# Converting float64 weights to float32: a scaled Abs and a maximum ahead of the shift in place of a guard behind the addition

## The chip, the cores and the metric

The kernel runs on one core of a Trainium2 chip. The metric is the time of the whole program on the device, in microseconds (us), as the median of several runs. The core's engines are TensorE (PE in the profile; PEld is its loading of weights), VectorE (DVE), ScalarE (ACT), GpSimd (POOL) and SyncE (SP), which here issues all transfers. Each works through its own queue in order.

## What is computed

```python
q_pool = q.reshape(B, H, S // 2, 2, D).mean(axis=3)        # B 4, H 8, S 1152, D 64
scores = np.matmul(q_pool, k.transpose(0, 1, 3, 2)) / np.sqrt(D)
attn = np.exp(scores - scores.max(-1, keepdims=True))
attn = attn / (attn.sum(-1, keepdims=True) + 1e-09)
x = np.matmul(attn, v)              # then as 2304 tokens of 512
h = x @ moe_w_in;  x = np.maximum(0.01 * h, h) @ moe_w_out          # 512 -> 2048 -> 512
h = x @ moe2_w_in; out = np.where(h > 0, h, np.exp(np.minimum(h, 0)) - 1) @ moe2_w_out
```

The attention inputs are float32. The four weight matrices arrive as float64, and the kernel computes in float32, so it converts them from their bits: each number is two 32-bit words, the low and the high one.

## The kernel before

The attention runs over 16 pairs (batch b of 4, head pair hp of 4). For each pair, `scores` (L452 to L463) multiplies queries by keys, takes the row maximum (DVE, L457 and L459) and the exponentials (ACT, L463); `transpose_p` (L475) turns the exponentials around and splits them into a rounded part and a rest (`psplit`, L261 to L267); `pv` (L496 to L509) multiplies by the values; `normalise` (L520 to L546) divides by the sums. L520 comes once for each pair, so its 16 instances mark how far the attention is.

The two layers of the MLP (`mlp`) run for each batch of 576 tokens over 16 blocks f of 128 hidden units: `up` (PE at L629, then the activation at L640 to L651), and after every four blocks `down` (PE at L667, sums on DVE at L680). Layer 0 and layer 1 of a batch are scheduled along with the attention of later batches. Each block needs 128 columns of w_in and 128 rows of w_out, tiles `wr` of 128 x 512, which `load_w` makes. When a layer's block is used for the first time (batch 0), `convert` makes it from the float64 words, and the result is also stored to memory (L328); later batches load that (`wr<-w`). ACT and POOL then split `wr` into `wi` or `wo` (L261, L267).

`convert` takes half a block (128 x 256) at a time, so there are 2 layers x 16 blocks x 2 matrices x 2 halves = 128 passes. Tiles `cr` (the raw words), `ct` and `cm` exist twice each (`CB = 2`). Per half the kernel before has six steps: on DVE the high word is shifted left by three and masked (L293), then its sign and top exponent bit are put in (L296); on ACT the low word is scaled by 2^-29 and so rounded (L299), and the magnitude of the high word, read as a float32, is taken into `cm` (L301); POOL adds the two words as integers (L303); on DVE the sum is multiplied by 1 or 0, as `cm` is at least `MIN_HI` or not, and written to `wr` (L305). That last step is the guard: numbers too small for the float32 exponent become zero.

The order on the engines is set by a planner inside the kernel (`Program`): every operation is entered with an engine, a cost in ns, a rank and the tiles that it reads and writes, and a list schedule decides the order in which they are emitted. A change of a step's engine, cost or inputs thus moves other instructions too. The costs of the steps concerned are

```python
def act(n, accum=False, sbuf=False):
    return 50 + 0.833 * n + (190 if accum else 0) + (43 if sbuf else 0)
def dve(n, fast=False):
    return 66 + (0.52 if fast else 1.05) * n
```

## Time and profile before

| | |
|---|---|
| three runs, median (lowest to highest) | 1552.36 us (1551.68 to 1554.34) |
| the profiled execution, first to last instruction (span) | 1550.8 us, 1.56 us under the median of the runs |
| PE busy | 1421.8 us, 92% |
| PEld busy | 1368.2 us, 88% |
| DVE busy | 1093.0 us, 70% |
| ACT busy | 1027.4 us, 66% |
| POOL busy | 844.7 us, 54% |
| granted TensorE clock, mean | 0.987 of full speed |

Busy shares are averages over a program whose first 590 us convert weights and whose rest does not; the shares of single stretches say more. Durations of an instruction include time in which it was begun and held up.

### The profile page before, as it was taken

What the parts mean: (1) busy time and instruction counts of PE and PEld (TensorE: products, weight loads), DVE (VectorE), ACT (ScalarE), POOL (GpSimd) and SP (SyncE); (2) the same over time, 40 slices, a digit from 0 to 9 for tenths busy, and PEclk for the clock granted to TensorE, in tenths of its full rate; (3) what the DMA queues carried; (4) which work ended last, traced back from release to release, by engine and by line L of the source; (5) the groups of instructions that cost most, each with busy time, mean ns of one, the idle gap of its engine ahead of it and who ended that gap; (6) DMA issues with size and microseconds to landing.
All of it is one profiled execution on the core that took longest, in us unless ns stands there. A gap on an engine that the chain in (4) does not pass through costs nothing.

```text
span 1550.8 us, 28885 instructions
## 1 busy us (share of the span) xinstructions
PE 1421.8 (92%) x10288; PEld 1368.2 (88%) x10288; DVE 1093.0 (70%) x2401; ACT 1027.4 (66%) x2773; POOL 844.7 (54%) x840
## 2 busy tenths in 40 slices
PE   5878899889888888999999999999999998899998
PEld 5777788878777788999999998999999998899897
DVE  6998898989999999656676767556676664224333
ACT  6998888777677777676667766776667652442442
POOL 5444256666666667444455556454554445566572
PEclk9999999999999999999999999999999999999999
DMA  4232124433334443222222222222221111322230
GB/s 145 90 114 86 40 79 139 128 114 124 125 119 136 142 133 115 83 77 60 69 74 70 79 77 63 93 73 61 70 71 42 55 55 56 92 76 82 69 89 31
DMA packets 82641, 135.58 MB, mean 87 GB/s; under 512 B 8512, under 2 KB 26944, under 8 KB 82496
## 3 DMA queue, kind: packets, MB, share of 16 engines
q1 hardware_dynamic: 82496, 133.73, 28.4%
q8 instruction: 81, 1.33, 0.4%
q14 instruction: 64, 0.52, 0.1%
HBM read 112.20 MB, written 21.50 MB: 86 GB/s over the span
## 4 chain that ended last, share of the span: by engine, by line
PE 50%; DVE 13%; ACT 3%; issue 2%; DMA 2%; POOL 2%; SPq 0%; ACTq 0%; POOLq 0%; DVEq 0%
PE h L667 15%; PE h L629 12%; PE s L452 5%; PE o L496 5%; PE t L475 4%; PE s L629 2%; DVE t L648 2%; PE s L667 2%; PE t L629 2%; DVE wr L305 2%; PE t L667 2%; DVE t L651 1%; PE t L373 1%; DVE pt L267 1%; DVE m L457 1%
## 5 line engine op out<-in xcount | busy, mean ns | idle before, releaser
L667 PE MATMUL h<-g,wo 128*128 128x288 f32 x2544 | 442.1, 305 | 18.5 <-DVE t L651 10.8
L629 PE MATMUL h<-xs,wi 128*128 128x288 f32 x2520 | 428.2, 305 | 22.9 <-DVE t L651 9.7
L629 PEld LDWEIGHTS h<-xs,wi 128*128 128x128 f32 x2520 | 362.8, 191 | 35.7 <-DVE t L651 15.4
L667 PEld LDWEIGHTS h<-g,wo 128*128 128x128 f32 x2544 | 368.6, 190 | 23.9 <-DVE t L651 13.0
L457 DVE TENSOR_REDUCE m<-s 128x1 f32<-128x384 f32 x432 | 231.3, 550 | 53.0 <-PE s L452 50.0
L267 POOL TENSOR_TENSOR g<-t,g 128x288 fp32r<-128x288 f32 x256 | 218.9, 863 | 89.3 <-ACT g L261 85.6
L261 ACT ACTIVATE pt<-t 128x384 fp32r<-128x384 f32 (+1 forms) x416 | 183.0, 455 | 126.1 <-PE t L475 116.4
L463 ACT ACTIVATE p<-s,m 128x384 f32<-128x384 f32 x432 | 248.4, 585 | 23.1 <-DVE m L459 22.7
L267 DVE TENSOR_TENSOR pt<-t,pt 128x384 fp32r<-128x384 f32 (+1 forms) x416 | 206.1, 508 | 56.6 <-ACT pt L261 55.0
L267 POOL TENSOR_TENSOR wo<-wr,wo 128x512 fp32r<-128x512 f32 x128 | 168.3, 1321 | 136.0 <-ACT wo L261 126.9
L452 PE MATMUL s<-kT,qT 128*128 128x384 f32 x768 | 195.2, 353 | 27.9 <-ACT p L463 27.6
L267 POOL TENSOR_TENSOR wi<-wr,wi 128x512 fp32r<-128x512 f32 x128 | 171.4, 1339 | 62.4 <-ACT wi L261 50.6
L475 PE MATMUL t<-ident,p 128*128 128x128 f32 x1116 | 181.1, 276 | 19.4 <-DVE pt L267 13.2
L496 PE MATMUL o<-pt,vn 128*128 128x256 f32 (+1 forms) x1152 | 190.7, 301 | 4.4 <-DVE pt L267 2.5
L496 PEld LDWEIGHTS o<-pt,vn 128*128 128x128 f32 x1152 | 164.4, 189 | 8.4 <-DVE pt L267 5.6
L261 ACT ACTIVATE g<-t 128x288 fp32r<-128x288 f32 x256 | 112.7, 446 | 88.1 <-DVE t L651 50.0
L475 PEld LDWEIGHTS t<-ident,p 128*128 128x128 f32 x1116 | 137.9, 142 | 31.5 <-DVE pt L267 14.1
L642 DVE SCALAR_TENSOR_TENSOR t<-t 128x288 f32<-128x288 f32 x128 | 90.6, 714 | 97.1 <-ACT t L640 96.6
L303 POOL TENSOR_TENSOR ct<-ct,cr 128x256 uint32<-128x256 uint32 x128 | 98.8, 773 | 109.5 <-DVE ct L296 41.0
L452 PEld LDWEIGHTS s<-kT,qT 128*128 128x128 f32 x768 | 126.1, 192 | 35.9 <-ACT p L463 34.5
L267 POOL TENSOR_TENSOR vn<-raw,vn 128x576 fp32r<-128x576 f32 x32 | 45.9, 1436 | 166.2 <-ACT vn L261 166.2
L261 ACT ACTIVATE wo<-wr 128x512 fp32r<-128x512 f32 x128 | 80.3, 630 | 83.0 <-PE h L667 51.8
(104 smaller groups left out, 2091.6 us busy)
## 6 DMA issues: line engine op xcount, KB each, us to landing
wr<-w SPq DMA_DIRECT2D x192, 256.0 KB, 2.7
cr<-in_moe_w_in_dram SPq DMA_DIRECT2D x64, 256.0 KB, 2.7
cr<-in_moe_w_out_dram SPq DMA_DIRECT2D x64, 256.0 KB, 2.7
w<-wr SPq DMA_DIRECT2D x64, 256.0 KB, 2.1
raw<-in_k_dram SPq DMA_DIRECT2D x32, 288.0 KB, 3.1
raw<-in_v_dram SPq DMA_DIRECT2D x32, 288.0 KB, 3.0
raw<-in_q_dram SPq DMA_DIRECT2D x32, 256.0 KB, 3.0
out_dram<-cr SPq DMA_DIRECT2D x16, 256.0 KB, 2.2
```

Source lines behind the costliest of these rows:

```text
L261: prog.add("ACT", act(n, sbuf=not psum), rank, lambda: A.activation(out=hi(), in_=src(), func=ACTF.Copy), w=[w], r=r)
L267: lambda: eng.tensor_tensor(out=lo(), in0=src(), in1=f32(hi()), op=ALU.subtract),
L303: prog.add("POOL", pool(CW), rank, lambda t=t, r=r: G.tensor_tensor(out=t.ap, in0=t.ap, in1=r[:, :, 0], op=ALU.add), w=[t], r=[t, (r, 0)])
L305: prog.add("DVE", dve(CW), rank, lambda n=n, t=t, mag=mag: V.scalar_tensor_tensor(out=dst[:, n:n + CW], in0=mag.ap, scalar=MIN_HI, in1=t.a ...
L452: PE.matmul(out=st[:, 0:384], lhsT=qa(a), rhs=kT[:, 384 * c:384 * c + 384], start=(i == 0), stop=(i == len(seq) - 1))
L457: prog.add("DVE", dve(384), rank - LR, lambda st=st, c=c: V.tensor_reduce(out=m[:, c:c + 1], in_=st[:, 0:384], axis=AX.X, op=ALU.max), w=[ ...
L463: prog.add("ACT", act(384, True), rank - LE, lambda c=c: A.activation(out=p[:, 384 * c:384 * c + 384], in_=banks[c][:, 0:384], func=ACTF.E ...
L475: PE.transpose(out=t[:, i, :], in_=p[:, (3 * c + i) * 128:(3 * c + i + 1) * 128], identity=ident)
L496: PE.matmul(out=o[:, 0:n], lhsT=vn[:, c, :], rhs=pt[th][:, a, c % 3, :], start=(c == 3 * ORDER[0] and a == 0), stop=(c == 3 * ORDER[2] + 2 ...
L629: PE.matmul(out=h[:, 0:HB], lhsT=wi[:, a, c, :], rhs=xs[c][:, e, cols], start=(c == 0 and a == 0 and e == 0), stop=(c == DC - 1 and a == 1))
L642: prog.add("DVE", dve(HB), rk, lambda t=t, g32=g32: V.scalar_tensor_tensor(out=g32.ap, in0=t.ap, scalar=0.01, in1=t.ap, op0=ALU.mult, op1= ...
L667: PE.matmul(out=y[:, 0:HB], lhsT=w[f][1][:, a, d * 128:(d + 1) * 128], rhs=g[f][:, e, cols], start=(f % FC == 0 and a == 0 and e == 0), st ...
```

## The change

The Abs pass on ACT now comes first. It multiplies by 2^16 and writes to `ct` in place of `cm`. A new DVE step takes the maximum of that and 2.0, in place. The shift by three works on the result in place, with a mask that keeps the top exponent bit; the next step adds the sign alone. The rounding of the low word is as before. POOL's addition now writes `wr` itself; the guard on DVE behind it and the tile `cm` are gone. Docstrings and comments, which the diff also removes, are left out here.

```diff
-    MIN_HI = 2.0 ** (112 - 127) * (1 + 2.0 ** -3)
...
-            mag = sb("cm", [128, CW], F32, CB)
...
-            prog.add("DVE", dve(CW, True), rank, lambda r=r, t=t: V.tensor_scalar(
-                out=t.ap, in0=r[:, :, 1], scalar1=3, scalar2=0x3FFFFFF8,
-                op0=ALU.logical_shift_left, op1=ALU.bitwise_and), w=[t], r=[(r, 1)])
+            prog.add("ACT", act(CW, sbuf=True), rank, lambda r=r, t=t: A.activation(
+                out=t.ap.bitcast(F32), in_=r[:, :, 1].bitcast(F32), func=ACTF.Abs, scale=2.0 ** 16),
+                w=[t], r=[(r, 1)])
+            prog.add("DVE", dve(CW, True), rank, lambda t=t: V.tensor_scalar(
+                out=t.ap.bitcast(F32), in0=t.ap.bitcast(F32), scalar1=2.0, scalar2=None, op0=ALU.max), w=[t], r=[t])
+            prog.add("DVE", dve(CW, True), rank, lambda t=t: V.tensor_scalar(
+                out=t.ap, in0=t.ap, scalar1=3, scalar2=0x7FFFFFF8,
+                op0=ALU.logical_shift_left, op1=ALU.bitwise_and), w=[t], r=[t])
             prog.add("DVE", dve(CW), rank, lambda r=r, t=t: V.scalar_tensor_tensor(
-                out=t.ap, in0=r[:, :, 1], scalar=0xC0000000, in1=t.ap,
+                out=t.ap, in0=r[:, :, 1], scalar=0x80000000, in1=t.ap,
                 op0=ALU.bitwise_and, op1=ALU.bitwise_or), w=[t], r=[(r, 1), t])
             prog.add("ACT", act(CW, sbuf=True), rank, lambda r=r: A.activation(
                 out=r[:, :, 0], in_=r[:, :, 0], func=ACTF.Copy, scale=2.0 ** -29), w=[(r, 0)], r=[(r, 0)])
-            prog.add("ACT", act(CW, sbuf=True), rank, lambda r=r, mag=mag: A.activation(
-                out=mag.ap, in_=r[:, :, 1].bitcast(F32), func=ACTF.Abs), w=[mag], r=[(r, 1)])
-            prog.add("POOL", pool(CW), rank, lambda t=t, r=r: G.tensor_tensor(
-                out=t.ap, in0=t.ap, in1=r[:, :, 0], op=ALU.add), w=[t], r=[t, (r, 0)])
-            prog.add("DVE", dve(CW), rank, lambda n=n, t=t, mag=mag: V.scalar_tensor_tensor(
-                out=dst[:, n:n + CW], in0=mag.ap, scalar=MIN_HI, in1=t.ap.bitcast(F32),
-                op0=ALU.is_ge, op1=ALU.mult), w=[(dst, n)], r=[t, mag])
+            prog.add("POOL", pool(CW), rank, lambda n=n, t=t, r=r: G.tensor_tensor(
+                out=dst[:, n:n + CW].bitcast(U32), in0=t.ap, in1=r[:, :, 0], op=ALU.add),
+                w=[(dst, n)], r=[t, (r, 0)])
```

In the changed kernel Abs is L292, the maximum L295, the shift L297, the and/or step L300, the low word's rounding L303 and POOL's addition L305. Most other lines stand one line earlier or where they stood.

The planner's order changes with the steps. On DVE during the sixth pair, before:

```order
L459 TENSOR_REDUCE m<-m 128x1
L305 SCALAR_TENSOR_TENSOR wr<-cm,ct 128x256
L293 TENSOR_SCALAR ct<-cr 128x256
L296 SCALAR_TENSOR_TENSOR ct<-cr,ct 128x256
L680 TENSOR_TENSOR acc<-h,acc 128x288
L305 SCALAR_TENSOR_TENSOR wr<-cm,ct 128x256
L293 TENSOR_SCALAR ct<-cr 128x256
L509 TENSOR_TENSOR xu<-o,tm 64x320
L296 SCALAR_TENSOR_TENSOR ct<-cr,ct 128x256
```

and of the change:

```order
L457 TENSOR_REDUCE m<-s 128x1
L295 TENSOR_SCALAR ct<-ct 128x256
L297 TENSOR_SCALAR ct<-ct 128x256
L300 SCALAR_TENSOR_TENSOR ct<-cr,ct 128x256
L266 TENSOR_TENSOR pt<-t,pt 128x3x128
L680 TENSOR_TENSOR acc<-h,acc 128x288
L295 TENSOR_SCALAR ct<-ct 128x256
L457 TENSOR_REDUCE m<-s 128x1
L297 TENSOR_SCALAR ct<-ct 128x256
L457 TENSOR_REDUCE m<-s 128x1
L300 SCALAR_TENSOR_TENSOR ct<-cr,ct 128x256
```

Where a half's third step, L305, stood behind POOL's addition and apart from the first two, the three steps of a half now stand together or with a step or two of the attention between them.

At the end of the conversions, on DVE behind the eighth pair's L520, before:

```order
L459 TENSOR_REDUCE m<-m 128x1
L522 TENSOR_SCALAR r<-r 128x9
L267 TENSOR_TENSOR pt<-t,pt 128x3x128
L305 SCALAR_TENSOR_TENSOR wr<-cm,ct 128x256
L524 RECIPROCAL r<-r 128x9
L399 TENSOR_SCALAR qs<-qs 128x256
L525 COPY rb<-r 128x512
```

and of the change, during the ninth pair:

```order
L459 TENSOR_REDUCE m<-m 128x1
L266 TENSOR_TENSOR pt<-t,pt 128x3x128
L295 TENSOR_SCALAR ct<-ct 128x256
L297 TENSOR_SCALAR ct<-ct 128x256
L300 SCALAR_TENSOR_TENSOR ct<-cr,ct 128x256
L266 TENSOR_TENSOR pt<-t,pt 128x3x128 x2
L457 TENSOR_REDUCE m<-s 128x1
L295 TENSOR_SCALAR ct<-ct 128x256
L262 CAST xs<-xu 128x288
L297 TENSOR_SCALAR ct<-ct 128x256
L262 CAST xs<-xu 128x288
L300 SCALAR_TENSOR_TENSOR ct<-cr,ct 128x256
```

The last L305 stood right behind the eighth pair's end, ahead of its L524; the last L300 now stands most of a pair later, among the casts (`xs<-xu`) that open layer 0 of batch 1. Twenty halves thus come behind the eighth L520 where one came before.

## Rows read from the trace of the kernel before

**Rows 1.** The page, the span in 40 equal slices: PE and DVE, busy tenths.

```profile
PE   5878899889888888999999999999999998899998
DVE  6998898989999999656676767556676664224333
```

**Rows 2.** Line L520 in three windows: count, duration ns min/median/max, first and last start.

```profile
L520 DVE TENSOR_REDUCE r<-sum x5: 171/172/173, 61.0 to 267.3; 128x9 f32<-128x27 f32 x5
...
L520 DVE TENSOR_REDUCE r<-sum x3: 170/172/183, 372.5 to 586.7; 128x9 f32<-128x27 f32 x3
...
L520 DVE TENSOR_REDUCE r<-sum x1: 183/183/183, 664.7 to 664.7; 128x9 f32<-128x27 f32 x1
```

**Rows 3.** Busy us by stretch: length, PE, PEld, DVE, ACT, POOL, clock, DMA, GB/s.

```profile
0.00:267.00 267.00, 216.62 (x1491) 198.35 (x1492) 231.83 (x552) 226.94 (x646) 125.01 (x135) 0.99 0.32 99
267.00:587.00 320.00, 274.52 (x1910) 256.31 (x1909) 301.28 (x651) 232.34 (x645) 208.49 (x218) 0.98 0.41 128
587.00:665.00 78.00, 71.28 (x534) 69.14 (x534) 56.57 (x122) 55.13 (x146) 46.62 (x45) 1.00 0.30 93
665.00:1551.00 886.00, 859.41 (x6359) 844.35 (x6357) 503.34 (x1080) 513.00 (x1337) 464.57 (x444) 0.99 0.24 69
```

**Rows 4.** Groups of DVE, 267 to 587: count, busy us, mean ns, idle before.

```profile
L305 DVE SCALAR_TENSOR_TENSOR wr<-cm,ct 128x256 f32<-128x256 f32 x91 | 71.7, 792 | 3.6 <-POOL ct L303 3.5
L296 DVE SCALAR_TENSOR_TENSOR ct<-cr,ct 128x256 uint32<-128x256 uint32 x89 | 46.5, 525 | 0.5
L457 DVE TENSOR_REDUCE m<-s 128x1 f32<-128x384 f32 x83 | 44.7, 546 | 2.3 <-PE s L452 2.2
L293 DVE TENSOR_SCALAR ct<-cr 128x256 uint32<-128x256 uint32 x89 | 44.0, 496 | 2.9 <-DMA cr<-in_moe_w_out_dram 1.9 <-DMA cr<-in_moe_w_in_dram 0.7
...
L524 DVE RECIPROCAL r<-r 128x9 f32<-128x9 f32 x3 | 0.6, 204 | 0.0
```

**Rows 5.** Tile ct, whole span: duration ns min/median/max.

```profile
L293 DVE TENSOR_SCALAR ct<-cr x128: 272/290/1380, 7.8 to 587.8; 128x256 uint32<-128x256 uint32 x128
L296 DVE SCALAR_TENSOR_TENSOR ct<-cr,ct x128: 402/415/1515, 9.4 to 588.5; 128x256 uint32<-128x256 uint32 x128
...
L305 DVE SCALAR_TENSOR_TENSOR wr<-cm,ct x128: 404/426/1680, 12.7 to 590.9; 128x256 f32<-128x256 f32 x128
```

**Rows 6.** Timeline, 481.5 to 485 us: start us, duration us.

```profile
481.66 0.41 DVE L305 SCALAR_TENSOR_TENSOR wr<-cm,ct 128x256 f32<-128x256 f32 x1
...
483.46 1.28 POOL L267 TENSOR_TENSOR wi<-wr,wi 128x512 fp32r<-128x512 f32 x1
483.59 1.44 DVE L305 SCALAR_TENSOR_TENSOR wr<-cm,ct 128x256 f32<-128x256 f32 x1
```

**Rows 7.** Lines L399 and L648, whole span: duration ns min/median/max.

```profile
L399 DVE TENSOR_SCALAR qs<-qs x32: 233/285/1497, 8.6 to 1143.5; 128x256 f32<-128x256 f32 x32
...
L648 DVE TENSOR_SCALAR t<-t x128: 293/332/1536, 426.2 to 1531.6; 128x288 f32<-128x288 f32 x128
```

**Rows 8.** Tiles cr and cm, ACT: duration ns min/median/max.

```profile
L299 ACT ACTIVATE cr<-cr x128: 420/440/480, 7.8 to 587.5; 128x256 uint32<-128x256 uint32 x128
...
L301 ACT ACTIVATE cm<-cr x128: 413/431/470, 8.1 to 588.6; 128x256 f32<-128x256 f32 x128
```

**Rows 9.** Timeline, 589 to 592 us, DVE: the last conversion step.

```profile
590.92 1.12 DVE L305 SCALAR_TENSOR_TENSOR wr<-cm,ct 128x256 f32<-128x256 f32 x1
```

**Rows 10.** 0 to 267 us: DVE's conversion groups, then a wait (us, times, longest).

```profile
L305 DVE SCALAR_TENSOR_TENSOR wr<-cm,ct 128x256 f32<-128x256 f32 x36 | 21.0, 589 | 2.0 <-POOL wo L267 1.2 <-POOL ct L303 0.8
L296 DVE SCALAR_TENSOR_TENSOR ct<-cr,ct 128x256 uint32<-128x256 uint32 x38 | 20.4, 544 | 0.1
L293 DVE TENSOR_SCALAR ct<-cr 128x256 uint32<-128x256 uint32 x38 | 18.5, 494 | 7.2 <-DMA cr<-in_moe_w_in_dram 7.1
...
PE s L452 <- ACT p L463: 29.1, 18, 4.6
```

**Rows 11.** The chain that ended last, in order of time, a piece: start us, us.

```profile
470.93 4.17 DMA cr<-in_moe_w_out_dram
```

## The prediction

> **What bounds the kernel now.** I read the page's slices first. TensorE (PE) is mostly at 8 tenths through the first sixteen slices (some 620 us) and at 9 nearly throughout behind them; VectorE (DVE) is at 8 or 9 in just those first slices [rows 1]. The float64 weights are converted there and nowhere else. The table of busy time by stretch cuts this at the attention pairs' normalisations, of which the first instruction is L520: the fifth at 267.3 us, the eighth at 586.7, the ninth at 664.7 [rows 2]. From 267 to 587, DVE is busy 301.28 of 320 us (94%) and PE 274.52 (86%); behind 665, PE is busy 859.41 of 886 (97%) and DVE 57% [rows 3]. So DVE sets the pace in the converting stretch, and PE behind it.
>
> The groups of DVE in that stretch show what its time goes to: the three conversion steps L305, L296 and L293 stand at 792, 525 and 496 ns on average [rows 4]. Undisturbed each is far shorter: 404, 402 and 272 ns at least [rows 5]. The timeline shows what the rest is. At 481.66 an L305 took 0.41 us; at 483.59 one took 1.44 us, beginning 0.13 us into a POOL subtraction of 1.28 us and ending 0.29 us behind it [rows 6]. POOL is busy 208.49 of these 320 us [rows 3], so DVE steps that work on SBUF alone, as these three do, often stand behind one of its operations; I take it that this is what L305's other 0.39 us are.
>
> The order of instructions tells where a gain would end: from about the ninth normalisation on, all five queues hold the same instructions in the same order in both kernels. So the stretch behind 665 us should last its 886 us again, and what is won or lost is won or lost ahead of it.
>
> **The change, part by part**, for each of the 128 half blocks.
>
> *Steps removed and added.* DVE keeps three steps. L305 (792 ns) goes; the maximum comes, one more step over 256 elements in SBUF with one input. No row shows a maximum there, but L399 is a float32 step of this shape and kind: 233 ns at least, 1497 at most; L648, in place over 288, 293 at least [rows 7]. So 0.27 us undisturbed. What it waits for POOL must be bounded. From below nothing, 0.27. From above L305's own wait, 792 - 404 = 0.39, so 0.66. I take L293's mean, 0.496, since the maximum takes L293's place as the first DVE step of a half. The shift, now behind the maximum, I put at 0.272 plus the wait that L296 has as a second step (525 - 415, its median [rows 5], = 0.11): 0.39; its ends are 0.272 and 0.496. The and/or step is L296 still: 0.525, ends 0.402 and 0.525. Sum 1.41 us for a half where 0.792 + 0.525 + 0.496 = 1.81 stand now; ends 1.17 and 1.68.
>
> *ScalarE (ACT)* has two passes over a half before and after, 440 and 431 ns at the median [rows 8], and POOL one addition; these totals don't change. What moves is the place: the Abs pass lay beside the DVE steps and now stands ahead of them, so the DVE steps of a half wait for it, and the addition and the half's input buffer with them. ACT is busy 73% of the stretch [rows 3]. On SP the store of a converted block waits for POOL instead of DVE, and the next loads stand behind it; it becomes ready a step sooner, which I count at nothing, since the load's buffer, the later one, decides.
>
> *Order.* The planner puts the conversions further apart. From the fifth normalisation to the last conversion step, DVE now has 661 instructions, 272 of them conversion; then 719, of which 282 (94 halves). So 437 other DVE steps stand there instead of 389. PE correspondingly has 366 matmuls, not 453, between the first product that uses the last converted block and the point from which both orders agree.
>
> *Sum.* The last conversion step begins at 590.92 us [rows 9], 324 us after 267. The durations of DVE's steps in that time add up to 350 us: 92 x 0.792 + 90 x 1.021 = 165, and 389 others at 0.477, which is 182.3 us over 382 steps in 23 groups from L457 to L524 [rows 4], = 186. That is 1.08 us of durations for each us, as neighbours overlap. With the change: 94 x 1.41 + 437 x 0.477 = 341, or 315 us at the same density: **9 us less**. Behind it 87 matmuls fewer remain; at the 534 in 78 us of that stretch [rows 3] **13 us less**. Ahead of 267 us, 36 halves at 0.589 + 0.544 + 0.494 = 1.63 [rows 10] become 34 at 1.41: 11 us of DVE. But there PE mainly waits for the exponentials (29.1 us for L463 [rows 10]), and DVE has 35 us to spare [rows 3]; I count **2 us**, ends 0 and 11. In all 24 us: 1550.8 - 24 = 1527, and 1.6 us lie between the span and the median of the runs (1552.36): 1529. With a half at 1.68 us the first term turns into 15 us more and the sum into 1550.8 + 15 - 13 = 1553, or 1554 as a median. With 1.17 the first term is 30 us less and, with the whole 11, the time 1499.
>
> **The rivals.** *The wait only moves.* The long L305 is POOL's doing: whatever DVE step stands in its place waits as long, so only 0.13 us for a half is saved, the difference of the undisturbed steps. That is the 1.68 of above: 1554. For it: L648 and L399 have been held up to 1536 and 1497 ns [rows 7]. Against it: L296, between the other two, waits only 0.11, so not each step meets a fresh operation of POOL, and the three steps of a half often stand together in the new order. The Trainium skill's page "SBUF — State Buffer", section "Who interferes with whom", speaks for this rival: a DVE operation in a two-port mode and a GpSimd operation exclude each other for a whole instruction, so the maximum takes the lock just as L305 did. By it alone the sum is this rival's 1554; rows 6 agree with its exclusion, and the row of L296 says that three such steps don't pay thrice.
>
> *The load's buffer sets the pace; the kernel gets slower.* Two input buffers take turns: 92 halves in 324 us are a turn of 7.04 us each. The Abs pass and the maximum lengthen the way from a buffer's landing to its release by 0.43 + 0.27 = 0.70 us. If half of that shows (the DVE step now often begins some time behind the landing), 47 turns of 7.39 us are 347 us, 23 more than now; less the 13 of the order, 1563. It decides from a turn of 7.21 us, where 47 turns eat up the 13 and 2 us. For it: the chain that ended last runs over a load of cr here and there [rows 11], and the planner itself spaces the halves out. Against it: DVE has only some 19 us idle in these 320, little of it ahead of L293, so the turn is stretched by DVE's queue, which gets shorter.
>
> *PE takes over.* If DVE's relief and the evener spread (some twenty halves move behind the eighth normalisation, where DVE is busy 56.57 of 78 us) are enough for PE to run at its later 97%, its 274.52 + 71.28 us up to 665 last 357 us instead of 398: 1511. Against it: DVE would then be busy above 90% too, and neither engine has kept that beside the other so far.
>
> **How the numbers follow.** The forecast of 1529 has 0.56; the wait that moves, at 1554, 0.13; the buffer's turn, at 1563, 0.17; PE's pace, at 1511, 0.14. The range goes from 1507, just past PE's pace, since 1499 needs every unknown at its best end, to 1563, the slow rival at its price; some 2 in 10 lie outside, mostly a slow rival that shows all of its 0.70 us. The forecast's own range is 1515 to 1543. A measurement of this kernel can tell 0.2%, 3.1 us, from no change. Faster by more is the forecast and PE's pace, less a little for its upper end: 0.69. Within it is the wait that moves: 0.13. Slower is the buffer's turn: 0.18 with rounding.
>
> **What would show it.** Right: the three DVE steps near 1.4 us a half, the maximum near 0.5; the ninth normalisation near 641 us; the stretch behind it again some 886 us; DVE still above 90% busy up to the last conversion. Wrong: a maximum near 0.66 (the wait moved), idle DVE ahead of the maximum, released by Abs or by a load (the buffer's turn), or PE at 95% and more ahead of the ninth normalisation. If the tail behind it changes by over 5 us, the argument from equal orders is wrong.

## The result: slower by 0.7%, and the profile after

The changed kernel takes 1562.95 us (median of four runs, 1559.95 to 1565.28) where the kernel before takes 1552.02 us in four runs: a ratio of 1.0072, 95% interval 1.0054 to 1.0089. The profiled execution of the changed kernel, the slowest of its four, spans 1563.5 us, 12.7 more than the 1550.8 of before; the medians are 10.9 apart.

Its slices, with the granted clock below, answer to [rows 1]:

```profile
PE   5887798989878888899999999999999998899998
DVE  7978788889998888656676677656776665224333
...
PEclk9999999999999997999999999999999999999999
```

One slice differs most: the sixteenth, 586 to 625 us, where the clock is at 7 tenths. Line L520 in three windows (count, duration ns, first and last start), as in [rows 2]:

```profile
L520 DVE TENSOR_REDUCE r<-sum x5: 170/172/174, 58.9 to 268.5; 128x9 f32<-128x27 f32 x5
L520 DVE TENSOR_REDUCE r<-sum x3: 170/175/184, 365.9 to 551.4; 128x9 f32<-128x27 f32 x3
L520 DVE TENSOR_REDUCE r<-sum x1: 183/183/183, 673.2 to 673.2; 128x9 f32<-128x27 f32 x1
```

The eighth normalisation comes 35 us sooner than before, and the ninth 8.5 us later. The first is no gain by itself, since the new order put less work ahead of it (PE has begun 3195 products at the eighth normalisation, 3397 before): a moved mark says nothing until the work between the marks is counted. So cut both kernels at equal times and count products. The kernel before, busy us by stretch (columns as in [rows 3]; the stretch ahead of 267 us is the first of [rows 3], with 1491 products):

```profile
267.00:551.00 284.00, 242.48 (x1679) 225.94 (x1678) 266.28 (x571) 203.83 (x569) 185.11 (x194) 0.98 0.40 126
551.00:601.00 50.00, 43.66 (x320) 41.72 (x319) 48.70 (x109) 38.53 (x103) 34.37 (x34) 1.00 0.47 143
601.00:631.00 30.00, 27.27 (x203) 25.88 (x202) 25.20 (x55) 18.43 (x53) 15.40 (x17) 1.00 0.19 59
631.00:665.00 34.00, 32.40 (x247) 31.91 (x246) 17.67 (x39) 26.69 (x72) 20.22 (x19) 1.00 0.32 101
```

The changed kernel, the same view:

```profile
0.00:267.00 267.00, 213.67 (x1458) 196.37 (x1459) 222.77 (x538) 221.73 (x631) 117.19 (x128) 0.97 0.30 93
267.00:551.00 284.00, 247.71 (x1736) 232.21 (x1736) 256.29 (x577) 210.71 (x587) 174.97 (x188) 0.98 0.38 120
551.00:601.00 50.00, 44.07 (x303) 40.19 (x302) 43.22 (x102) 34.86 (x93) 31.38 (x33) 0.94 0.43 132
601.00:631.00 30.00, 21.91 (x114) 20.29 (x114) 24.77 (x55) 18.94 (x51) 18.98 (x21) 0.75 0.43 137
631.00:665.00 34.00, 31.32 (x230) 30.52 (x231) 18.49 (x44) 19.28 (x52) 17.42 (x16) 1.00 0.37 110
```

By 267 us the changed kernel is 33 products behind; from there to 551 it does 57 more (1736 against 1679), and at 601 us the two stand level: 1491 + 1679 + 320 = 3490, and 1458 + 1736 + 303 = 3497. Then 30 us follow in which it does 114 products where 203 were done. At 203 in 30 us, the 89 missing are 13 us: **in the balance, the whole loss lies between 601 and 631 us.** Products differ in size, from 128 to 384 columns; counted in columns, from PE's groups by form, the two also stand level at 601 us (891,936 before, 890,368 now), and the 30 us hold 51,968 and 30,208. What follows is nearly equal: 17 products fewer up to 665 us (1,600 columns), and the stretch from the ninth normalisation to the end takes 890.3 us against 886.1, but it holds 6393 products (from 673 us, the row below) against 6359, at 7.2 a us some 4.7 us' worth.

```profile
673.00:1564.00 891.00, 863.83 (x6393) 848.87 (x6391) 506.41 (x1083) 517.08 (x1347) 468.37 (x448) 0.99 0.24 69
```

What DVE does up to the last conversion step, its groups from 268 to 626 us, against [rows 4]:

```profile
L295 DVE TENSOR_SCALAR ct<-ct 128x256 f32<-128x256 f32 x94 | 53.6, 572 | 9.4 <-ACT ct L292 8.3 <-ACT cr L303 0.4 <-POOL kn L266 0.2
L300 DVE SCALAR_TENSOR_TENSOR ct<-cr,ct 128x256 uint32<-128x256 uint32 x95 | 51.0, 538 | 1.2
L297 DVE TENSOR_SCALAR ct<-ct 128x256 uint32<-128x256 uint32 x94 | 43.0, 459 | 1.1
```

A half costs 0.572 + 0.538 + 0.459 = 1.57 us of DVE instead of 1.81. Undisturbed the steps are short, as the tile ct shows (duration ns min/median/max, first and last start), beside [rows 5]:

```profile
L292 ACT ACTIVATE ct<-cr x128: 419/436/480, 7.7 to 621.7; 128x256 f32<-128x256 f32 x128
L295 DVE TENSOR_SCALAR ct<-ct x128: 235/294/1544, 8.2 to 622.8; 128x256 f32<-128x256 f32 x128
L297 DVE TENSOR_SCALAR ct<-ct x128: 275/294/1495, 9.7 to 624.0; 128x256 uint32<-128x256 uint32 x128
L300 DVE SCALAR_TENSOR_TENSOR ct<-cr,ct x128: 404/420/1499, 10.2 to 625.1; 128x256 uint32<-128x256 uint32 x128
```

The last conversion step stands at 625.1 us, not at 590.9 [rows 9]. So the steps are cheaper, and yet they end 34 us later.

What PE meets in the bad stretch is seen in its timeline (start us, us, engine, line, tiles, in brackets the idle time before and what ended it):

```profile
606.72 3.36 PE L629 MATMUL h<-xs,wi 128*128 128x288 f32 x24
609.92 2.26 PE L452 MATMUL s<-kT,rem 128*128 128x384 f32 x12
612.02 0.82 PE L475 MATMUL t<-ident,p 128*128 128x128 f32 x6
617.15 1.54 PE L475 MATMUL t<-ident,p 128*128 128x128 f32 x6 [4.32 <-DVE pt L266]
...
622.10 5.27 PE L629 MATMUL h<-xs,wi 128*128 128x288 f32 x24
```

For 4.32 us PE waits with its next transpose for DVE's step on `pt`. DVE's timeline says what stands in front of that step:

```profile
609.83 1.26 DVE L399 TENSOR_SCALAR qxs<-qxs 128x64 f32<-128x64 f32 x1 [1.41 <-POOL qxs L397]
611.01 0.87 DVE L295 TENSOR_SCALAR ct<-ct 128x256 f32<-128x256 f32 x1
...
614.19 0.45 DVE L295 TENSOR_SCALAR ct<-ct 128x256 f32<-128x256 f32 x1
...
615.59 1.04 DVE L300 SCALAR_TENSOR_TENSOR ct<-cr,ct 128x256 uint32<-128x256 uint32 x1
616.55 0.55 DVE L266 TENSOR_TENSOR pt<-t,pt 128x384 fp32r<-128x384 f32 x1
```

DVE waits 1.41 us for POOL, then steps stand held up (L399 1.26, L295 0.87, L300 1.04 us), among them the conversions of two halves, and behind all that comes `pt`. ACT had rounded its part of that tile by about 614.0, so some 2.5 of the 4.32 us are DVE's queue. Between the fifth and the ninth normalisation this wait of PE is 25.4 us in the changed kernel (us in all, times, longest):

```profile
PE t L475 <- DVE pt L266: 25.4, 15, 4.6
...
ACT ct L292 <- DMA cr<-in_moe_w_in_dram: 12.1, 13, 3.3
DVE ct L295 <- ACT ct L292: 8.3, 14, 1.4
ACT ct L292 <- DMA cr<-in_moe_w_out_dram: 6.0, 12, 0.9
```

and 10.5 us in the kernel before:

```profile
PE t L475 <- DVE pt L267: 10.5, 15, 1.9
```

Of the other three rows, DVE's wait of 8.3 us for Abs is new. ACT waited for the loads before the change too, with its rounding of the low word (L299, 11.0 us from 267 to 665); now Abs meets them first, and it is 18.1 us.

### The profile page after: what moved, and what is told of

It reads as the page before. It is cut to its first block, busy times and chain, and to the rows that moved or that the text cites. A ratio compares the mean times of both kernels' runs of the same rounds, so it can differ in the third digit from the quotient of the medians.

```text
span 1563.5 us, 28873 instructions
## 1 busy us (share of the span) xinstructions
PE 1430.3 (91%) x10288; PEld 1376.0 (88%) x10288; DVE 1076.6 (69%) x2401; ACT 1029.4 (66%) x2773; POOL 835.5 (53%) x840
## 4 chain that ended last, share of the span: by engine, by line
PE 57%; DVE 19%; ACT 7%; issue 6%; POOL 3%; DMA 3%; ACTq 0%; SPq 0%; POOLq 0%; DVEq 0%
PE h L667 15%; PE h L629 13%; PE s L452 7%; PE o L496 7%; PE t L475 5%; PE s L629 2%; PE s L667 2%; DVE ct L295 2%; DVE t L648 2%; DVE m L457 2%; DVE ct L300 2%; DVE pt L266 2%; DVE t L642 2%; DVE ct L297 2%; PE t L373 2%
## 5 line engine op out<-in xcount | busy, mean ns | idle before, releaser
L667 PE MATMUL h<-g,wo 128*128 128x288 f32 x2544 | 436.0, 303 | 13.5 <-DVE t L651 11.1
L629 PE MATMUL h<-xs,wi 128*128 128x288 f32 x2520 | 420.8, 304 | 10.2 <-DVE t L651 3.2
L629 PEld LDWEIGHTS h<-xs,wi 128*128 128x128 f32 x2520 | 361.5, 191 | 20.6 <-DVE t L651 8.0
L496 PE MATMUL o<-pt,vn 128*128 128x256 f32 (+1 forms) x1152 | 195.6, 306 | 6.3 <-DVE pt L266 5.7
L496 PEld LDWEIGHTS o<-pt,vn 128*128 128x128 f32 x1152 | 168.8, 194 | 10.6 <-DVE pt L266 10.4
L305 POOL TENSOR_TENSOR wr<-ct,cr 128x256 uint32<-128x256 uint32 x128 | 97.2, 760 | 123.8 <-DVE ct L300 49.2
```

Of the source, the lines that this page charges most:

```text
L305: prog.add("POOL", pool(CW), rank, lambda n=n, t=t, r=r: G.tensor_tensor(out=dst[:, n:n + CW].bitcast(U32), in0=t.ap, in1=r[:, :, 0], op=A ...
L496: PE.matmul(out=o[:, 0:n], lhsT=vn[:, c, :], rhs=pt[th][:, a, c % 3, :], start=(c == 3 * ORDER[0] and a == 0), stop=(c == 3 * ORDER[2] + 2 ...
L629: PE.matmul(out=h[:, 0:HB], lhsT=wi[:, a, c, :], rhs=xs[c][:, e, cols], start=(c == 0 and a == 0 and e == 0), stop=(c == DC - 1 and a == 1))
L667: PE.matmul(out=y[:, 0:HB], lhsT=w[f][1][:, a, d * 128:(d + 1) * 128], rhs=g[f][:, e, cols], start=(f % FC == 0 and a == 0 and e == 0), st ...
```

## The experiments

The theory after this reading: the new steps relieve DVE, but the **planner's order** for them loses it again. In its plan a half's way through two buffers is longer (load, Abs, maximum, shift, and/or, addition), so it spaces the halves out, twenty of them into the ninth pair, where PE then waits. The rivals: it is **the two buffers on the chip** (each half's turn is longer), it is **the wait for Abs**, or it is **the maximum**, a step that costs as much as it saves. All ratios are to the kernel before, run beside them, whose medians were 1550.2 to 1552.6 us.

### e1: a third buffer for the raw words

```diff
+    REAL = {'cr': 3}
...
-        return prog.buf(tag, bufs, lambda: sp.tile(shape, dt, tag=tag, name=tag, bufs=bufs))
+        return prog.buf(tag, bufs, lambda: sp.tile(shape, dt, tag=tag, name=tag, bufs=REAL.get(tag, bufs)))
```

> The changed kernel, all queues in the same order, but the raw words' tile cr has three buffers in memory instead of two (the planner still reckons with two). Turn theory (two raw buffers, each held from its load to POOL's addition, set the pace since the way through Abs and the maximum became longer): the 3 us of a load leave the turn, the last and/or step moves from 625 to about 595 us and the time falls to some 1535 us. Order theory (the planner's order, with twenty halves in the ninth pair, is what costs): the order is the same, so 1560 to 1565. Load theory (DVE's steps of 1.57 us a half, not 1.41, set the pace): 1560 to 1565.

1555.60 us, ratio 1.0025 (1.001 to 1.004): some 7 us of the loss come back. The ninth pair still takes 119.1 us where it took 121.8. The runs in the changed kernel's order (e1, e3, e4, e8, e9, e14) give PE the same products in the same sequence, so the bad stretch can be followed even where a run is ahead in time: its 114 products last 29.9 us in the change and 29.7 in e1. The turn of the buffers is part of the loss, not the larger part.

### e2: the new steps in the order of before

```diff
+            def first(r=r, t=t):
+                A.activation(
+                    out=t.ap.bitcast(F32), in_=r[:, :, 1].bitcast(F32), func=ACTF.Abs, scale=2.0 ** 16)
...
+            prog.add("DVE", dve(CW, True), rank, first, w=[t], r=[(r, 1)])
...
+            prog.add("ACT", act(CW, sbuf=True), rank, lambda: None, w=[mag], r=[(r, 1)])
...
+            prog.add("DVE", dve(CW), rank, lambda: None, w=[(dst, n)], r=[t, mag])
```

> The changed kernel's six steps, emitted where the planner puts the steps of the kernel before (Abs, maximum and shift in the place of the old shift, the addition in the place of the old one, nothing in the guard's place); wr has one buffer more so that the addition may write it early. Turn theory: the order wants 92 halves by the eighth normalisation again, with a longer turn: 1565 to 1585, slower than the change. Order theory: as before or somewhat faster, 1540 to 1553. Load theory: DVE has 0.24 us a half less than before, 1535 to 1550.

1589.35 us, 1.0246 (1.0222 to 1.0271), much slower. The order of before has no place for Abs ahead of the DVE steps, so each Abs stands too late in ACT's queue, and DVE waits 41.8 us for it between the fifth and the ninth normalisation:

```profile
DVE ct L298 <- ACT ct L296: 41.8, 58, 2.4
```

The run does not separate order and steps, since it adds a wait of its own. It shows that the old order, with each Abs put in beside the shift, doesn't carry the new steps.

### e3 and e4: without the maximum, and with the maximum beside the others

e3 leaves the maximum out, so that words below its bound are converted wrongly:

```diff
-            prog.add("DVE", dve(CW, True), rank, lambda t=t: V.tensor_scalar(
-                out=t.ap.bitcast(F32), in0=t.ap.bitcast(F32), scalar1=2.0, scalar2=None, op0=ALU.max), w=[t], r=[t])
+            prog.add("DVE", dve(CW, True), rank, lambda: None, w=[t], r=[t])
```

> The changed kernel in its own order without the maximum on DVE (so numbers below the smallest float32 exponent are not caught). Turn theory: the way is shorter by 0.27 to 0.57 us, 47 turns give 13 to 27 us: 1536 to 1550. Load theory: 0.57 us x 94 halves off a queue that sets the pace, 40 us or more: 1510 to 1525. Order theory: 1560 to 1565.

In e4 the maximum runs, but reads the raw word and writes a tile that nobody reads; the shift then reads what Abs wrote:

```diff
+            prog.add("DVE", dve(CW, True), rank, lambda r=r: V.tensor_scalar(
+                out=scrap, in0=r[:, :, 1].bitcast(F32), scalar1=2.0, scalar2=None, op0=ALU.max), w=[t], r=[t])
```

> The changed kernel in its own order, with the maximum still on DVE at its place in the queue, but taken of the raw high word and written to a scrap tile, so that the shift reads Abs directly (numbers below the smallest float32 exponent are not caught). DVE has as much to do as in the change, and the maximum no longer waits for Abs. Turn theory: the maximum still stands ahead of the shift in the queue but may run while Abs does, so up to 0.3 us of the way goes: 1549 to 1563. Load theory and order theory: 1560 to 1565.

e3: 1537.35 us, 0.991 (0.9886 to 0.9933). e4: 1558.79 us, 1.0046 (1.003 to 1.0062). The two differ by the maximum's time on DVE alone, and that is 21 us of 1559. It is less than the step's own duration in e4, 94 times 537 ns = 50 us, and one reason stands in the groups of e3, 265 to 650 us:

```profile
L299 DVE SCALAR_TENSOR_TENSOR ct<-cr,ct 128x256 uint32<-128x256 uint32 x94 | 59.1, 630 | 1.3
L296 DVE TENSOR_SCALAR ct<-ct 128x256 uint32<-128x256 uint32 x94 | 46.8, 499 | 6.5 <-ACT ct L292 5.7 <-POOL g L266 0.4
```

With the maximum gone, the and/or step is 630 ns instead of 538 and the shift 499 instead of 459: a quarter of the saving moves to the steps that are left. And even here the ninth pair takes 119.1 us and its bad 114 products 28.8, so what makes it long is not this step: 19 of e3's 27 us (by the profiled spans) lie ahead of the eighth normalisation, which comes at 532.2 us instead of 551.4.

### e8: no wait for Abs

Abs and the maximum both run into tiles that nobody reads, and shift and and/or step read the raw word with the masks of before, so that nothing guards against small numbers:

```diff
-                out=t.ap.bitcast(F32), in_=r[:, :, 1].bitcast(F32), func=ACTF.Abs, scale=2.0 ** 16),
+                out=scrap2, in_=r[:, :, 1].bitcast(F32), func=ACTF.Abs, scale=2.0 ** 16),
...
-                out=t.ap, in0=t.ap, scalar1=3, scalar2=0x7FFFFFF8,
+                out=t.ap, in0=r[:, :, 1], scalar1=3, scalar2=0x3FFFFFF8,
...
-                out=t.ap, in0=r[:, :, 1], scalar=0x80000000, in1=t.ap,
+                out=t.ap, in0=r[:, :, 1], scalar=0xC0000000, in1=t.ap,
```

> The changed kernel in its own order and with as many steps on each engine, but Abs and the maximum write scrap tiles, and the shift reads the raw high word, as it does in the kernel before (numbers below the smallest float32 exponent are not caught). So DVE no longer waits for Abs. If waiting for ACT costs the time: 1545 to 1552. Order theory and load theory: 1556 to 1560, as with the maximum beside.

1558.67 us, 1.0052 (1.0035 to 1.0069). The wait for Abs is worth some 3 to 4 us, and the two intervals (this one and the change's) overlap, so it may be nothing or twice that; e4, in which only the maximum is freed from Abs, measured the same. The ninth pair stays at 120.5 us, and the bad 114 products at 29.7.

### e5, e6 and e7: the planner's settings

e5, the changed kernel told that transfers are short:

```diff
-    LATENCY = {"PE": 200, "SP": 2500,
+    LATENCY = {"PE": 200, "SP": 1500,
```

> The changed kernel, but the planner reckons 1500 ns instead of 2500 for a load, so that its plan of a half is again no longer than that of the kernel before; the steps and buffers are the change's. Its order has 64, 92 and 124 halves at the ends of the sixth, seventh and eighth pair, near the kernel before (65, 95, 127), against 59, 80 and 108 in the change. Order theory (the twenty halves that the planner puts into the ninth pair cost the time): 1540 to 1550. Turn theory (the buffers' turn on the chip sets the pace): the chip cannot follow such an order, 1565 or more. Load theory: as the change, 1560 to 1565.

1573.95 us, 1.0144 (1.0112 to 1.0175): conversions as early as before, in a plan that the two buffers don't follow. Abs waits 43.6 us for loads between the fifth and the ninth normalisation, 18.1 in the change. e6, the kernel *before* told that transfers are long (3200), so that its halves are spaced nearly like the change's:

> The kernel before with all its steps, but the planner reckons 3200 ns for a load, so that it puts the halves further apart, as in the change: 62, 87 and 114 at the ends of the sixth, seventh and eighth pair, and PE's matmuls nearly as in the change. Order theory: slower than before, 1560 to 1570. Turn theory: on the chip the turn is the old one and there is more room for it, 1545 to 1553. Load theory: DVE has the same work, 1550 to 1555.

1547.57 us, 0.998 (0.9967 to 0.9993): with the steps of before the wider spacing does no harm on the whole. But its ninth pair is slow too:

```profile
554.10:656.80 102.70, 89.52 (x621) 85.02 (x620) 82.85 (x174) 68.49 (x185) 62.26 (x62) 0.95 0.41 124
```

That is 6.0 products a us, where the kernel before does 6.8 ([rows 3], 587 to 665) and the changed one 5.8 (707 in its 121.8 us). What e6 loses there it has won ahead: from 267 to 551 us it does 1803 products, 124 more than before, and the changed kernel only 57 more. So a ninth pair with late conversions is slow with either set of steps, and the spacing alone doesn't make the kernel slower. e7, the changed kernel with three buffers in plan and memory:

```diff
-    CB = 2
+    CB = 3
...
+    REAL = {'r': 1}
```

(`REAL` gives tile `r` of the normalisation one buffer, for which the memory was short.)

> The changed kernel with three buffers of the raw words and of ct, in memory and in the plan. The order has 69, 103 and 128 halves at the ends of the sixth, seventh and eighth pair: the conversions are done earlier than in the kernel before. Order theory and turn theory: 1530 to 1545, faster than both. Load theory: DVE's conversions are packed more tightly where DVE is full, 1555 to 1570.

1545.81 us, 0.9968 (0.9954 to 0.9982), 17 us faster than the change; the ninth pair takes 79.8 us and does 7.0 products a us. Against e1, which has a third buffer of the raw words in memory alone, the plan, with a third `ct`, is worth 10 us.

### e9 and e14: the last twenty halves left almost bare

For the twenty halves in the ninth pair Abs, maximum, shift and and/or step are left out, and the addition takes the raw word (their weights come out wrong):

```diff
+            bare = len(halves) >= 108
...
-            prog.add("DVE", dve(CW, True), rank, lambda t=t: V.tensor_scalar(
+            prog.add("DVE", dve(CW, True), rank, lambda t=t, bare=bare: bare or V.tensor_scalar(
...
+                out=dst[:, n:n + CW].bitcast(U32), in0=r[:, :, 1] if bare else t.ap, in1=r[:, :, 0], op=ALU.add),
```

> The changed kernel in its own order, but the last 20 halves, those that stand in the ninth pair, are left almost bare: no Abs, no maximum, no shift and no and/or step; the load, the low word's rounding and POOL's addition stay, so that these twenty halves of layer 1's weights come out wrong. If the conversions themselves, by DVE's time or by the wait in a half's way, cost the ninth pair its time (20 x 1.57 us = 31 us of DVE), it falls from 122 us to about 90 and the kernel to about 1530. If it is the order (the blocks that are left for the ninth pair and the casts of batch 1 that stand among them, with TensorE waiting for activations and its clock falling), the ninth pair stays at 112 to 120 us and the kernel above 1550.

e14 has a third raw buffer in memory as well (the edit of e1):

> The changed kernel in its own order with the last 20 halves bare (no Abs, maximum, shift and and/or step for them, so that these halves of the weights come out wrong) and a third buffer for the raw words, in memory alone. Each of the two alone gave some 7 to 11 us. If the ninth pair's loss is the conversions' DVE steps and the two buffers' turn together, both gains add: 113 us for the ninth pair become 104 or less, 1540 to 1545 in all. If what is left is the order of attention and MLP, the ninth pair stays at 110 to 114 and the kernel at 1546 to 1553.

e9: 1552.95 us, 1.0001 (0.9979 to 1.0023). e14: 1546.91 us, 0.9969 (0.9952 to 0.9985). The stretch with the bad 114 products (and two or three at its ends) in the change, in e9 and in e14:

```profile
602.20:632.10 29.90, 21.34 (x116) 19.99 (x115) 24.67 (x55) 18.38 (x50) 18.26 (x21) 0.77 0.45 141
595.60:621.00 25.40, 18.41 (x116) 17.02 (x115) 17.84 (x38) 17.41 (x47) 17.33 (x21) 0.92 0.54 170
593.20:617.80 24.60, 18.14 (x117) 16.71 (x116) 16.93 (x38) 17.11 (x46) 16.67 (x21) 0.93 0.52 165
```

At the pace of before (203 products in 30 us) 114 products take 17 us, so of some 13 us lost there 4.5 come back without the late DVE steps, and 5.3 with the third buffer too. The whole ninth pair is 113 us in e9 and 110 in e14, of 121.8; at the 6.8 products a us of before its 707 would take some 104. So the late conversions are a third to a half of what goes wrong there. The rest remains when they cost almost nothing; that it lies in the order of the attention's and the MLP's steps around them is what is left, not what a run shows. e9's time equals that of the kernel before, but e9 leaves out most of the work of 20 halves.

### e10: the guard removed and nothing put in its place

The kernel before in its own order, with Abs and guard left out (small numbers would not become zero), and `wr` with a fifth buffer in memory:

```diff
+            prog.add("ACT", act(CW, sbuf=True), rank, lambda: None, w=[mag], r=[(r, 1)])
+            prog.add("POOL", pool(CW), rank, lambda n=n, t=t, r=r: G.tensor_tensor(
+                out=dst[:, n:n + CW].bitcast(U32), in0=t.ap, in1=r[:, :, 0], op=ALU.add), w=[t], r=[t, (r, 0)])
+            prog.add("DVE", dve(CW), rank, lambda: None, w=[(dst, n)], r=[t, mag])
```

> The kernel before in its own order without the guard: the Abs pass and the multiplication by the guard are left out, and POOL's addition writes the converted block itself; numbers below float32's exponents would not become zero. It shows what taking the third step off DVE is worth if nothing is put in its place and nothing moves: by the forecast's count 0.79 us less for each of 92 halves behind the fifth normalisation, 73 us of durations, 67 us of time if DVE alone sets the pace; by 'the wait only moves' 37 us. As TensorE was 86% busy there it can't give more than some 40: expected 1510 to 1520, and below 1505 only if the limit was DVE all along. If it stays above 1535, DVE was not what bounded the converting stretch, and the forecast's first step fails at its root.

1515.47 us, 0.9767 (0.9742 to 0.9792), 36 us less. One DVE step is gone, but so is ACT's Abs pass, and POOL's addition ends the conversion, so the run alone doesn't give all of it to DVE; e3 against e4, which differ in one DVE step only, gave 21 us for a shorter step. Together they say that DVE set much of the pace. The remaining two steps, 259 to 560 us, against [rows 4]:

```profile
L298 DVE SCALAR_TENSOR_TENSOR ct<-cr,ct 128x256 uint32<-128x256 uint32 x90 | 56.9, 634 | 0.8
L295 DVE TENSOR_SCALAR ct<-cr 128x256 uint32<-128x256 uint32 x90 | 48.2, 537 | 11.4 <-DMA cr<-in_moe_w_in_dram 6.8 <-DMA cr<-in_moe_w_out_dram 3.8 <-POOL wr L304 0.5
```

They grow from 525 to 634 and from 496 to 537 ns: 0.15 us of the 0.39 that L305 waited moves on to them, and 0.64 us of its 0.79 are saved.

### e11, e12 and e13: which part of the plan

e11 is e7 with transfers of 3600 ns in the plan:

```diff
-    LATENCY = {"PE": 200, "SP": 2500,
+    LATENCY = {"PE": 200, "SP": 3600,
...
-    CB = 2
+    CB = 3
```

> The changed kernel with three input and word buffers, in the plan and in memory, as in the run before of this kind (1546), and with the planner's cost of a transfer at 3600 ns in place of 2500, so that the conversions stand a little further apart (66, 96 and 128 halves by the sixth, seventh and eighth normalisation instead of 69, 103 and 128). If the plan's order decides, and its best is between that of the three buffers and the spread one, the time is 1538 to 1545 and so beats both kernels; if the third buffer already gave what there was, it is 1546 to 1550.

1529.15 us, 0.9862 (0.9842 to 0.9881), better than expected and faster than both kernels. e12 and e13 instead tell the planner how long the three DVE steps really take, e12 with two buffers, e13 on top of e11:

```diff
-            prog.add("DVE", dve(CW, True), rank, lambda t=t: V.tensor_scalar(
+            prog.add("DVE", 470, rank, lambda t=t: V.tensor_scalar(
...
-            prog.add("DVE", dve(CW), rank, lambda r=r, t=t: V.scalar_tensor_tensor(
+            prog.add("DVE", 535, rank, lambda r=r, t=t: V.scalar_tensor_tensor(
```

> The changed kernel with two buffers as it is; only the planner's costs of the three conversion steps on DVE are raised to what the profile shows for them (470 ns for the maximum and the shift, 535 for the and/or step, in place of 199 and 335). The order then leaves as many halves for the ninth pair as the change's own (108 by the eighth normalisation) but puts the attention's steps less tightly behind the conversions. If the loss in the ninth pair comes from the planner's short costs, the kernel gains 8 to 15 us, to 1548 to 1555. If it comes from the two buffers of its plan, so that the last twenty halves stand in the ninth pair whatever they cost, it stays at 1558 to 1575.

> The kernel with three buffers and 3600 ns for a transfer in the plan (1529), with the raised costs of the three DVE steps (470, 470 and 535 ns) as well. More products are then placed ahead of the fifth normalisation (1666 against 1574), and the order has 76, 107 and 128 halves at the sixth, seventh and eighth. If honest costs help wherever the buffers allow it, it is 1515 to 1527; if the first pairs can't carry more conversions, 1530 to 1545.

e12: 1561.20 us, 1.007 (1.0045 to 1.0096), the time of the change. e13: 1536.96 us, 0.9913 (0.9887 to 0.9939), slower than e11. True costs in the plan help neither. In e7 and e11 three buffers do, but they stand in memory as well as in the plan. In e11 a half costs even more than in the changed kernel (groups of DVE, 265 to 573 us: 516 + 542 + 578 ns = 1.64 us):

```profile
L302 DVE SCALAR_TENSOR_TENSOR ct<-cr,ct 128x256 uint32<-128x256 uint32 x90 | 52.0, 578 | 0.8
L299 DVE TENSOR_SCALAR ct<-ct 128x256 uint32<-128x256 uint32 x90 | 48.8, 542 | 1.0
L297 DVE TENSOR_SCALAR ct<-ct 128x256 f32<-128x256 f32 x89 | 46.0, 516 | 2.1 <-ACT ct L294 1.7
```

What differs is where they stand and what PE waits for. The last and/or step comes at 570.3 us, as the tile ct of e11 shows:

```profile
L302 DVE SCALAR_TENSOR_TENSOR ct<-cr,ct x128: 404/419/1677, 10.2 to 570.3; 128x256 uint32<-128x256 uint32 x128
```

PE's wait for `pt`, from its fifth to its ninth normalisation, is small:

```profile
PE t L477 <- DVE pt L268: 7.0, 12, 2.4
```

and from 601 to 631 us it does 199 products at full clock, as the kernel before did 203:

```profile
601.00:631.00 30.00, 27.30 (x199) 26.19 (x198) 23.19 (x52) 16.66 (x47) 13.26 (x13) 1.00 0.18 60
```

Not all of e11's gain lies there. Its last 6346 products, all behind the conversions, take 872 us, and 884 in the changed kernel and in the one before: 12 of the 37 us between the profiled spans come from the tail, whose order the new plan changes too.

### e15 and e16: `pt` let ahead in the queues

The last question was whether PE's wait for `pt` is the cause or only goes with the order. Behind the planner's schedule, up to the last conversion, the two steps that split a transposed tile are put forward as far as what they read allows; e15 moves ACT's and DVE's step, e16 DVE's alone:

```diff
+        for i in sorted(self.early, key=lambda i: at[i]):
+            if at[i] < last:
...
+                k, n = max(key[o] for o in d)
+                key[i] = min(key[i], (k, n + 1))
...
+                prog.early += [len(prog.ops) - 2, len(prog.ops) - 1]
```

> The changed kernel with two buffers and its own plan; up to the last conversion the two steps that split a transposed tile (ScalarE's rounding of pt and VectorE's rest of pt) are then put as far forward in their queues as what they read allows, so ahead of conversion steps, casts and activations that stand there. If TensorE's wait for pt causes the loss, that wait falls from 25 us to about 10, the 114 products between 601 and 631 become 170 or more and the kernel gains 8 to 13 us, to 1550 to 1555. If the wait is only where the late conversions show, TensorE waits as long for the blocks or activations and the kernel stays at 1559 to 1566.

> As the run before it, but VectorE's step alone is put forward, as far as right behind ScalarE's rounding, which stays in its place. If pt is late because conversion steps stand ahead of it on VectorE, most of the gain comes from this alone (1551 to 1557); if it is late because ScalarE rounds late, behind Abs passes that wait for loads, the kernel stays within 3 us of the change.

Both are clear misses: 1675.42 us, 1.0786 (1.0764 to 1.0807), and 1603.61 us, 1.0326 (1.031 to 1.0341). In e15 PE's wait for `pt` falls to 2.6 us, but the wait only changes sides, as the waits from 267 to 700 us show:

```profile
DVE pt L281 <- ACT pt L275: 63.8, 69, 2.6
```

A step put ahead of its inputs stops all that is queued behind it: DVE now waits 63.8 us, 69 times, for ACT's rounding. PE's wait for `pt` is a sign of the loss that goes with this order; that it is the cause was not shown.

## Why the prediction was wrong

The forecast was 1529 us, faster; measured are 1562.95, slower. In the forecast's own terms its sum was 2 + 9 + 13 us less; in the profiled executions the first term is 1.2 us more, the second 33.0 more, and the third 21.5 less.

**DVE bounds the converting stretch: right in the main.** e3 against e4, with one DVE step less and all else in place, shows 21 us; e10, in which ACT's Abs pass goes too, 36.

**A half costs 1.41 us: low, it measured 1.57.** The maximum was put at 0.496 and measured 0.572, the shift at 0.39 and measured 0.459, the and/or step at 0.525 and measured 0.538. So a half saves 0.24 us, where the forecast had 0.40 and the rival of the moving wait 0.13. 0.15 of L305's wait of 0.39 moved on in e10; that rival thus had a part of it, not all. The lower end of a half, 1.17, doesn't follow from its parts: 0.27 + 0.272 + 0.402 are 0.94, and 1.17 has the maximum at its 0.496; nothing measured hangs on it. The Trainium skill's page "SBUF — State Buffer", section "Who interferes with whom", says that a DVE operation in a two-port mode, or one with two inputs in SBUF (the memory on the chip that the engines share) beside a GpSimd operation that reads SBUF, and the GpSimd operation exclude each other. The steps of e3 and e10 that grew agree with it, the two-input and/or step most, but their 0.13 and 0.15 us a half are only part of the 0.34 and 0.39 that the removed steps had waited.

**The sum, "9 us less" for the last conversion: this is the step that failed.** It took 92 and 94 halves with their neighbours at one density, 1.08 us of durations in each us, forecast the last step 315 us behind the fifth normalisation, and found it at 356.6. So where 9 us less were forecast for this term, 33 more came. The durations from 268 to 626 us are 147.6 us for the conversions and 211 for the 440 other steps, 359 in all where 341 was forecast. That is 18 us more, from the dearer half above all. The larger part is the density: 359 us of durations in 358 us is 1.00, and at 1.08 it would have been 332. DVE's idle time, summed over its groups, went from 18.9 us (267 to 592, before) to 39.7, and 28.0 of these stand ahead of the attention's and the MLP's steps (11.9 before), not of the conversions. The forecast had taken it for granted that DVE keeps its density when its conversions stand among 437 other steps instead of 389. It didn't: those other steps wait for PE and ACT, and near the end of the conversions PE in turn waits for them. e11, with 370 other steps ahead of the last conversion, is back at 329 us of durations in 306, 1.08. But that the greater number of other steps takes the density is not shown: e10, in the order of before and with 384 of them, has 1.00 as well (296 us of durations in 297). A DVE that is relieved waits more for the others; how much of the loss is that and how much the order stays open.

**"13 us" for 87 products fewer behind the last conversion: more than kept.** From its last conversion step on the changed kernel lasts 938.4 us (1563.5 - 625.1), where the kernel before lasts 959.9 (1550.8 - 590.9), 21.5 less, with 160 products fewer. What was lost was lost ahead of that step. The 57 products that the changed kernel gains between 267 and 551 us are used up by 601: it starts 33 behind and loses 17 from 551 to 601. Then the 30 us at the end of the conversions lose 89.

**"2 us" ahead of the fifth normalisation: wrong in sign.** It comes at 268.5 against 267.3, and by 267 us 33 products fewer are done, at the later pace of 7.2 a us some 5 us' worth. No run was made to ask why; PE's wait for the exponentials there is 30.3 us, 29.1 before [rows 10].

**The tail that doesn't change: right,** once the products are counted. The last 6346 products have the same sequence in both kernels and take 884.4 us now, 884.1 before.

**The rivals.** The load's buffer gave the time, 1563, but only part of the mechanism, and that the time fits is luck: its turns were to cost 23 us more and cost 33, and the 13 us of the order were 21.5. Its sign, idle DVE ahead of the maximum, is there (9.4 us, 8.3 of them for Abs), and the turn is 356.6 / 47 = 7.59 us where 7.39 was forecast; yet a third buffer in memory gives back 7 us (e1) and freedom from Abs 4 (e8). Its larger effect went through the planner, which counts the same two buffers. With three in the plan the change is 17 us faster (e7), and with a longer transfer as well it is 34 us faster (e11). PE's pace was not reached: PE was busy 247.71 of the 284 us up to 551, 87%, hardly more than before. DVE was busy 89% up to the last conversion, not above 90%.

What stays open is which steps of the order make the 30 us. The late conversions are a third to a half of the loss there (e9, e14); the rest, and whether PE's wait for `pt` causes or only shows it, was not settled. Nor is e11's gain over the kernel before the steps' alone, since the kernel before with its tile `cm` left no room for a third buffer, and so was not run with one.

## What to carry to other kernels

Where a planner inside the kernel sets the order, its model of the buffers can cost more than the steps that an edit changes: here the same arithmetic ran in 1529 to 1574 us as the number of buffers and the planner's cost of a transfer were varied. Don't carry the density of a bound engine over to a stretch in which it has been relieved or its work is spread among steps that wait for others; count work done by equal times, in both kernels, and look for the stretch in which the counts part. And when a wait shows up in the profile, moving the waited-for step to the front of an in-order queue may simply put the wait on the other side.

## What was not expected of the hardware

The granted clock was low where PE had been kept waiting. Busy us in the changed kernel from 601 to 641 us, by 10 us:

```profile
601.00:611.00 10.00, 10.00 (x58) 9.72 (x59) 6.97 (x16) 8.27 (x24) 7.59 (x9) 0.75 0.53 161
611.00:621.00 10.00, 4.52 (x23) 3.45 (x22) 9.57 (x24) 5.29 (x13) 4.98 (x7) 0.76 0.41 129
621.00:631.00 10.00, 7.40 (x36) 7.12 (x35) 8.22 (x17) 5.38 (x15) 6.42 (x7) 0.73 0.35 121
631.00:641.00 10.00, 9.52 (x70) 9.44 (x71) 7.63 (x20) 4.64 (x14) 8.31 (x8) 1.00 0.40 109
```

The means of 0.73 to 0.76 are part of the time at the lower of two levels, 1.2 instead of 2.4 GHz. One fall comes at 599 us, in a stretch (591 to 601) in which PE was busy 8.48 of 10 us, and lasts to 606; the other comes at 616, in the wait of 4.32 us, and lasts to 626. In the timeline above 24 products of L629 take 5.27 us at 622.10, for the most part at the lower level, and 3.36 us at 606.72, at the higher. A starved stretch is thus dearer than its idle time: PE is idle 8.1 us in these 30 (30 - 21.91) while 13 us' worth of products are missing. In e11 and before the change the same 30 us have a clock of 1.00.
